# Job scaling on GpSimd and the second four jobs between the first FFN products

## Chip, core and metric

The kernel runs on one core of a Trainium2 chip. The metric is device time in microseconds of one execution. A core has the engines TensorE (PE, with weight loads PEld), VectorE (DVE), ScalarE (ACT) and GpSimd (POOL), each with an instruction queue of its own worked off in order, and SyncE (SP), whose queue issues nearly all DMAs here.

## What is computed

```python
# q, k, v: (8, 8, 576, 64)
scores = q @ k.T / sqrt(64)
gamma  = 1 - 2.0 ** (-5 - arange(8))            # one per head
Dmat   = where(i >= j, gamma ** (i - j), 0)     # decay, causal
x = ((scores * Dmat) @ v)                        # -> (4608, 512)
xn = x / sqrt(mean(x*x, -1) + 1e-6) * rms_g
g  = xn @ w_gate;  val = xn @ w_val              # 512 -> 1536
out = (g * sigmoid(g) * val) @ w_out             # 1536 -> 512
```

Everything is float32 on the chip; the FFN's weights come as float64 and are rounded by the kernel itself, with integer operations.

## The kernel before

**Jobs.** The attention is cut into 32 jobs, one for a batch and a pair of heads (`jobs`), numbered from 0. A sequence of 576 is worked in nine chunks of 64: scores within a chunk and states (k times v of a chunk) by `scores` and `states` on TensorE, decay and causal mask by `weigh` (two L317 instructions on VectorE, to `ret`), a running sum of states by `sums` (L331, L333), then `values` (v times `ret`, L354) and `carried` (sums times q, L374) into the same PSUM banks `av`, and at last x by a multiplication with a table of powers of gamma (L396). `slot(j)` issues `values(j-1)`, `scores(j)`, `states(j)`, `weigh(j)`, `sums(j)` and `carried(j-1)` in an interleaved order; `close(j)` issues the last two parts of a job alone. Between `values` and `carried` stands a tiny instruction that writes `tick` and that the first `carried` product waits for: on POOL for the first eight jobs (L361), on ScalarE from then on (L363).

**First eight jobs (`FIRST`), batches 0 and 1.** `load_first` and `load_tails` bring q, k and v in wide rows into the room of h and of the ring; `turn(j)` transposes q and k on TensorE (L233, L227, L242) and ScalarE copies the result out (L238, L249); `scale_v` multiplies v by powers of gamma on ScalarE (four L265 instructions).

**Later jobs.** `fetch(j)` issues thirteen DMAs on SP: q and k in pieces of 32x32 (`qraw`, `kraw`, one buffer each, so that the next job's load waits for `prepare` of this one), then k, v and vt. `prepare(j)` transposes qraw and kraw on VectorE (two L256) and scales v on ScalarE.

**Norm of a slice of 512 tokens.** `square` (ScalarE), `gather` (VectorE), `norm_1` (means on TensorE L447, r on VectorE, power -0.5 on POOL L453), `diagonals` (four L461), `norm_2` (one product L513 to rb and four L515 on x).

**Weights.** They come in 36 halves, in the order of `halves`: two sets of W_gate/W_val blocks (four halves each), one slice of W_out (four halves), and so on, six sets and three slices. For each, `rounding` issues three steps: the exponent of the next half (one L872 on VectorE, two passes L865 on ScalarE, popped by `act`), the mantissa (L887, L891, L895) and the join (L912). `weights(n)` issues n steps, `weights_to(n)` as many as bring n halves. After a set or slice, POOL builds sums of blocks (L923), and `store_blocks` stores them (L948) to `w_up_blocks` or `w_out_blocks`, from which `refill` loads pieces into the ring (L564). Each join also issues the raw load of the half five further on. From the first FFN product on, exponents and mantissas lie in PSUM banks, which all parts of the kernel share (eight).

**First FFN product of slices 0 and 1.** `up_plain(u, k)` makes four steps of four 128x512 products (L655) for slice u and set k; each step ends in a Silu on ScalarE (even k, L663) or a product with h on VectorE (odd k, L661). Twelve pairs (u, k) make 48 steps, counted by `now`; behind each step the loop in `start` issues what stands at that number: jobs 8 to 11 as `prepare` and `fetch` (28, 36, 41, 44, 46) and `slot` (34, 40, 42, 45), `close(11)` at 47, and weights. After (0, 5), which is step 39, come the rest of the weights, the stores of the last slice of W_out and the first reload, `refill(1)`; after (1, 4), step 43, `refill(2)`.

**Then** `across(0)` and `across(1)` make the second FFN product of slices 0 and 1 (L735), and slices 2 to 8 follow, each with `up` (L594) and `across`; the jobs of the next slice lie between them.

The order of instructions on every engine is that in which `start` issues them (`manual_schedule`); semaphores follow from the tiles. Scores of job j need kT and qT; a step needs the halves of its set.

Of the kernel before, what the change touches and what calls it, by code (L numbers as in the profile page):

```python
# [10 lines left out]
F32 = mybir.dt.float32  # L11
U32 = mybir.dt.uint32
AF = mybir.ActivationFunctionType
ALU = mybir.AluOpType
# [8 lines left out]
def _decay_tables(H, D):  # L23

    pairs = _gamma(H).reshape(H // 2, 2).T
    rows = np.repeat(pairs, D, axis=0)
    pos = np.arange(L)
    p = np.concatenate([pos, pos])  # L30
    gq = rows[:, :, None] ** (pos + L) / np.sqrt(D)
    t = pairs.T[None] ** -p[:, None, None], rows**L, gq, np.roll(gq, D, axis=0)
# [9 lines left out]
def kernel(  # L42
# [67 lines left out]
    gx = const.tile([P, NHP, L], F32, name="gx")  # L110
    gv = const.tile([P, NHP, 2], F32, name="gv")
    gc = const.tile([P, NHP], F32, name="gc")
    tick = const.tile([1, 1], F32, name="tick")
    rms_g = const.tile([P, NHP], F32, name="rms_g")
    rms_k = const.tile([P, NHP], F32, name="rms_k")
# [135 lines left out]
    def prepare(j):  # L251
# [5 lines left out]
            d[nm + "T"] = t  # L257
        scale_v(j)

    def scale_v(j):  # L260
        d = st[j]
        hp = jobs[j][1]
        for e in range(2):
            for t in (d["v"][:, :, e], d["vt"][:, e]):
                nc.scalar.activation(  # L265
                    out=t, in_=t, func=AF.Copy, scale=gv[: t.shape[0], hp, e : e + 1]
                )
# [79 lines left out]
    def values(j):  # L347

        d = st[j]
        av = d["av"] = [bank(f"av_{j}_{i}") for i in range(2)]  # L350
        for c in range(NC):
            i, odd = divmod(c, 2)
            for e in range(2):
                mm = nc.tensor.matmul(  # L354
                    av[odd][column(j, odd, e), i * L : i * L + L],
                    lhsT=d["v"][side(odd), i, e] if c < NC - 1 else d["vt"][:, e],
                    rhs=d["ret"][side(odd), e, i],
                    start=(c < 2), stop=False, skip_group_check=True,
                )
        if j < FIRST:  # L360
            d["valued"] = nc.gpsimd.memset(tick, 0.0)  # L361
        else:
            d["valued"] = nc.scalar.copy(out=tick, in_=mhalf[:1])  # L363
        follow(d["valued"], mm)

    def carried(j):

        d = st[j]
        b, hp = jobs[j]
        av = d["av"]  # L370
        for c in range(1, NC):
            i, odd = divmod(c, 2)
            for e in range(2):
                mm = nc.tensor.matmul(  # L374
                    av[odd][column(j, odd, e), i * L : i * L + L], lhsT=d["sum"][side(e), c - 1],
                    rhs=d["qT"][side(e), c * L : c * L + L],
                    start=False, stop=(c >= NC - 2), skip_group_check=True,
                )
                if c == 1 and e == 0:
                    follow(mm, d["valued"])  # L380
        cut = U // L - b
        for u, c0, c1, o in ((b, 0, cut, b * L), (b + 1, cut, NC, 0)):
            if u not in x_of:
                x_of[u] = xp.tile([P, NHP, U], F32, tag="x", name=f"x_{u}")
            x = x_of[u][:, hp, o : o + (c1 - c0) * L].rearrange("p (c k) -> p c k", k=L)
            for first in (c0, c0 + 1):
                i, odd = divmod(first, 2)
                n = -(-(c1 - first) // 2)
                if n <= 0:
                    continue  # L390
                moves = [(slice(0, P),) * 2]
                if column(j, odd, 0) != side(0):
                    moves = [(side(e), column(j, odd, e)) for e in range(2)]
                for to, at in moves:
                    g = (gq if to == at else gx)[at, hp].unsqueeze(1)
                    nc.vector.tensor_tensor(  # L396
                        out=x[to, first - c0 :: 2],
                        in0=av[odd][at, i * L : (i + n) * L].rearrange("p (c k) -> p c k", k=L),
                        in1=g.to_broadcast([at.stop - at.start, n, L]), op=ALU.mult,
                    )  # L400
        st[j] = {}
# [599 lines left out]
    def start():  # L1001

        nonlocal in_psum
        tables = list(zip((causal, gv, gc, gq, gx), (_causal_table(), *_decay_tables(H, D))))
# [10 lines left out]
        for i in (1, 0, 2):  # L1015
            table(i, nc.scalar)
        for j in range(FIRST):
            load_first(j)
            if j == 0:
                load_tails(0, range(2))  # L1020
                table(3, nc.sync)
            elif j == 1:
                load_tails(0, range(2, H))
                load_half(0, nc.sync)
            elif j in (2, 4, 5, 7):
                load_half({2: 1, 4: 2, 5: 3, 7: 4}[j], nc.sync)
            if j == 3:
                nc.sync.dma_start(out=rms_g, in_=moe_rms_g.rearrange("(c p) -> p c", p=P))
                load_tails(1, range(H))
                table(4, nc.sync)  # L1030
        turn(0, 1)
        scale_v(0)
        squares = []
        for j in range(FIRST):
            slot(j, rest=(j > 0))
            if j + 1 < FIRST:
                turn(j + 1)
            if squares:
                gather(*squares.pop())
            for i in ((1,), (2,), (3,), (4, 5), (6,), (7,), (), ())[j]:  # L1040
                scale_v(i)
            if j:
# [12 lines left out]
        gather(*squares.pop())  # L1055
        fetch(FIRST)
        in_psum = True
        now = 0
        for u, k in (
            (0, 0), (1, 0), (0, 1), (1, 1), (0, 2), (1, 2), (0, 3), (1, 3), (0, 4), (0, 5), (1, 4),  # L1060
            (1, 5),
        ):
            weights_to(READY[k] - 2)
            for i, _ in enumerate(up_plain(u, k)):
                if now == 0:
                    close(FIRST - 1)
# [24 lines left out]
                act(2)  # L1091
                if i == 1:
                    weights_to(READY[k])
                now += 1
            sets_used[k] += 1
            if (u, k) == (0, 5):
                weights_to(len(halves))
                store_blocks(len(halves) + 9)
                refill(1)
            elif (u, k) == (1, 4):  # L1100
                refill(2)
                for f in range(0, NH, 2):
                    differences(0, f)
                inner_sums(0, 0)
                inner_sums(0, 1)
# [82 lines left out]
```

## Time and profile before

| | |
|---|---|
| median of 12 runs | 1151.53 us (1149.22 to 1154.15) |
| the profiled execution | 1151.71 us, span 1149.9 us |
| TensorE busy | 1103.3 us (96%) |
| VectorE, ScalarE, POOL busy | 823.4, 247.5, 399.0 us |
| mean granted TensorE clock | 0.985 |
| slices 0 to 2 of 40 (28.7 us each) | PE busy 8, 7, 8 tenths |
| slice 8 (230 to 259 us) | PE busy 5 tenths |

The span is what the trace shows from the first to the last instruction; the execution's own time has 1.8 us more around it. A row of the timeline has start and duration in us, engine, line, operation, out<-in, count, and in brackets the idle time before it and who ended it. Matmul records come as two to a float32 matmul, so four products of a step are eight records. "issue" as a releaser is a wait that nothing in the profile explains. SPq rows are DMA issues on SP; a DMA lands some us later.

### The profile page before, as it was taken

What the parts mean: (1) busy time and instruction counts of PE and PEld (TensorE: products, weight loads), DVE (VectorE), ACT (ScalarE), POOL (GpSimd) and SP (SyncE); (2) the same over time, 40 slices, a digit from 0 to 9 for tenths busy, and PEclk for the clock granted to TensorE, in tenths of its full rate; (3) what the DMA queues carried; (4) which work ended last, traced back from release to release, by engine and by line L of the source; (5) the groups of instructions that cost most, each with busy time, mean ns of one, the idle gap of its engine ahead of it and who ended that gap; (6) DMA issues with size and microseconds to landing.
All of it is one profiled execution on the core that took longest, in us unless ns stands there. A gap on an engine that the chain in (4) does not pass through costs nothing. (4 is left out here: it accounts for less than half of the span.)

```text
span 1149.9 us, 24145 instructions
## 1 busy us (share of the span) xinstructions
PE 1103.3 (96%) x10086; PEld 919.4 (80%) x10086; DVE 823.4 (72%) x1426; ACT 247.5 (22%) x501; POOL 399.0 (35%) x328
## 2 busy tenths in 40 slices
PE   8789999958999999999999999999999999999997
PEld 6644444437998889888988898889988998898897
DVE  3788979848786778677957794779576944593465
ACT  3633434301102130223012301220122111201110
POOL 0022625534751028201830174016500660173035
PEclk8999999979999999999999999999999999999999
DMA  9645688588886886597768874897576565475461
GB/s 211 161 96 211 229 286 286 171 249 252 312 316 212 232 258 237 167 215 224 263 201 218 249 270 163 201 226 292 186 187 235 193 218 205 150 279 173 156 240 38
DMA packets 255421, 249.22 MB, mean 217 GB/s; under 512 B 193104, under 2 KB 213840, under 8 KB 249168
## 3 DMA queue, kind: packets, MB, share of 16 engines
q1 hardware_dynamic: 253728, 247.11, 68.8%
q8 instruction: 79, 1.29, 0.5%
q10 hardware_dynamic: 1584, 0.56, 0.2%
q14 instruction: 30, 0.25, 0.1%
HBM read 217.55 MB, written 30.08 MB: 215 GB/s over the span
## 5 line engine op out<-in xcount | busy, mean ns | idle before, releaser
L706 POOL TENSOR_TENSOR vi<-h 128x384 f32<-128x384 f32 x64 | 79.6, 1259 | 502.9 <-DVE h L613 453.6
L655 PE MATMUL up<-x,ring 128*128 128x512 f32 x384 | 169.1, 600 | 1.3 <-DVE x L515 0.9
L594 PE MATMUL x<-x,ring 128*128 128x256 f32 x672 | 161.5, 383 | 0.9 <-issue 0.9
L594 PE MATMUL w<-sums,ring 128*128 128x256 f32 x672 | 159.3, 380 | 0.0
L594 PE MATMUL z<-x,ring 128*128 128x256 f32 x672 | 158.7, 379 | 0.0
L655 PEld LDWEIGHTS up<-x,ring 128*128 128x128 f32 x384 | 73.0, 192 | 92.3 <-issue 86.2
L594 PEld LDWEIGHTS z<-x,ring 128*128 128x128 f32 x672 | 127.7, 190 | 19.9 <-issue 2.9
L594 PEld LDWEIGHTS w<-sums,ring 128*128 128x128 f32 x672 | 127.3, 190 | 17.4
L594 PEld LDWEIGHTS x<-x,ring 128*128 128x128 f32 x672 | 125.1, 190 | 18.5 <-issue 1.1
L594 PE MATMUL y<-sums,ring 128*128 128x256 f32 x336 | 79.4, 379 | 0.0
L601 DVE TENSOR_TENSOR h<-u,w 128x512 f32<-128x512 f32 x42 | 28.9, 687 | 65.0 <-PE w L594 48.1
L807 POOL TENSOR_TENSOR vi<-vi 128x512 f32<-128x512 f32 (+1 forms) x56 | 67.1, 1211 | 22.3 <-DVE vi L753 19.7
L594 PEld LDWEIGHTS y<-sums,ring 128*128 128x128 f32 x336 | 63.8, 190 | 8.7
L601 DVE TENSOR_TENSOR u<-m,y 128x512 f32<-128x512 f32 x42 | 28.8, 685 | 50.3 <-PE y L594 50.3
L620 ACT COPY m<-x 128x512 f32<-128x512 f32 x42 | 24.6, 585 | 181.5 <-PE x L594 181.5
L333 DVE SCALAR_TENSOR_TENSOR sum<-sum,gc,s 128x64 f32<-128x64 f32 x192 | 53.9, 281 | 6.8
L615 ACT ACTIVATE h<-h 128x512 f32<-128x512 f32 x63 | 39.5, 629 | 84.0 <-DVE h L601 84.0
L749 ACT COPY vi<-xo 128x512 f32<-128x512 f32 x18 | 10.5, 586 | 207.2 <-PE xo L735 177.6
L923 POOL TENSOR_TENSOR vi<-vi 128x512 f32<-128x512 f32 (+1 forms) x24 | 40.4, 1683 | 35.5 <-DVE vi L912 14.7
L317 DVE SCALAR_TENSOR_TENSOR ret<-s,causal 128x320 f32<-128x320 f32 x64 | 28.8, 484 | 26.7 <-PE s L284 22.3
L601 DVE TENSOR_TENSOR u<-u,z 128x512 f32<-128x512 f32 x42 | 28.8, 687 | 26.7 <-PE z L594 25.7
L923 POOL TENSOR_TENSOR ring<-ring 128x512 f32<-128x512 f32 x24 | 30.5, 1274 | 49.9 <-DMA w_up_blocks<-ring 44.5
(248 smaller groups left out, 2020.1 us busy)
## 6 DMA issues: line engine op xcount, KB each, us to landing
ring<-w_out_blocks SPq DMA_DIRECT2D x63, 1344.0 KB, 6.7
ring<-w_up_blocks SPq DMA_DIRECT2D x42, 1792.0 KB, 7.8
w_out_blocks<-vi SPq DMA_DIRECT2D x21, 448.0 KB, 6.6
out_dram<-vi SPq DMA_DIRECT2D x64, 128.0 KB, 2.9
qraw<-in_q_dram SPq DMA_DIRECT2D x96, 72.0 KB, 5.2
kraw<-in_k_dram SPq DMA_DIRECT2D x96, 72.0 KB, 3.2
k<-in_k_dram SPq DMA_DIRECT2D x48, 128.0 KB, 2.9
v<-in_v_dram SPq DMA_DIRECT2D x48, 128.0 KB, 2.8
```

Source lines behind the costliest of these rows:

```text
L317: nc.vector.scalar_tensor_tensor(out=ret[:, e], in0=s[e][:, : n * L].rearrange("p (c k) -> p c k", k=L), scalar=float(_gamma(H)[2 * hp + e ...
L333: nc.vector.scalar_tensor_tensor(out=t[:, c], in0=t[:, c - 1], scalar=gc[:, hp : hp + 1], in1=part, op0=ALU.mult, op1=ALU.add,)
L594: nc.tensor.matmul(ps[:, i * HU : i * HU + HU], lhsT=w[:, PLACE[blk], c, i * P : i * P + P], rhs=t_of[u][blk][:, c], start=(start and i == ...
L601: nc.vector.tensor_tensor(out=o, in0=a, in1=pairs_of(ps), op=ALU.add)
L615: nc.scalar.activation(out=o, in_=c, func=AF.Silu)
L620: nc.scalar.copy(out=s1, in_=pairs_of(x_))
L655: nc.tensor.matmul(ps, lhsT=w[:, PLACE[blk], c % 2, i * P : i * P + P], rhs=x_of[u][:, c], start=(c == 0), stop=(c == NHP - 1),)
L706: eng.tensor_tensor(out=o, in0=a, in1=b, op=op)
L749: nc.scalar.copy(out=o, in_=ps)
L807: eng.tensor_tensor(out=t[:, :, o], in0=t[:, :, x], in1=t[:, :, y], op=ALU.add)
L923: nc.gpsimd.tensor_tensor(out=t[o], in0=t[x], in1=t[y], op=op)
```

## The change

**Scaling.** For the first eight jobs `scale_first(j)`, on POOL, replaces `scale_v(j)`: four tensor_tensor multiplications in place, on q (by a new table gf that holds the powers that x was multiplied by before), its tail, v and its tail; each has a broadcast second operand. It comes ahead of `turn(j)`, two jobs ahead in most places. x then needs no factor: in `carried`, ScalarE copies `av` to x for j < FIRST, and VectorE does nothing there. `values` writes `tick` for these jobs on VectorE instead of POOL.

**First loads.** gf is the first table on ScalarE's queue; gq and gx come last on SP instead of among the jobs; tails of batch 1 follow job 4, weight halves 0 to 3 follow jobs 2 to 5.

**Order.** Jobs 0 to 3 run as slots and are closed alone; then job 4's slot, the norm of slice 0 and two halves of weights; jobs 5, 6 and 7 stand behind steps 0, 1 and 2 of `up_plain`, `close(7)` behind step 3, the norm of slice 1 behind steps 4 and 5, `fetch(8)` behind step 6. The order of pairs begins (0, 0), (0, 1), (1, 0), (1, 1), not (0, 0), (1, 0), (0, 1), (1, 1). Behind every step stand three weight steps (a whole half), where one stood behind the first four and two or three in turn behind the others. The stores of the last slice of W_out move from behind (0, 5) to behind (1, 4), and so behind `fetch(11)` on SP; both first reloads follow them there, ahead of `fetch(12)`.

```diff
+    def scale_first(j):
+        d = st[j]
+        hp = jobs[j][1]
+        n = NFULL
+        for t, g in (
+            (d["q"], gf[:, hp, :, :n]), (d["qt"], gf[:TAIL, hp, :, n]),
+            (d["v"].rearrange("p c e d -> p e c d"), gv[:, hp].unsqueeze(2)), (d["vt"], gv[:TAIL, hp]),
+        ):
+            g = g.unsqueeze(len(g.shape)).to_broadcast(list(t.shape))
+            nc.gpsimd.tensor_tensor(out=t, in0=t, in1=g, op=ALU.mult)
...
         if j < FIRST:
-            d["valued"] = nc.gpsimd.memset(tick, 0.0)
+            d["valued"] = nc.vector.memset(tick, 0.0)
...
                 for to, at in moves:
+                    if j < FIRST:
+                        nc.scalar.copy(
+                            out=x[:, first - c0 :: 2],
+                            in_=av[odd][:, i * L : (i + n) * L].rearrange("p (c k) -> p c k", k=L),
+                        )
+                        continue
...
-        turn(0, 1)
-        scale_v(0)
-        squares = []
-        for j in range(FIRST):
+        scale_first(0)
+        turn(0, 1)
+        scale_first(1)
+        for j in range(NHP):
             slot(j, rest=(j > 0))
-            if j + 1 < FIRST:
-                turn(j + 1)
             if squares:
                 gather(*squares.pop())
-            for i in ((1,), (2,), (3,), (4, 5), (6,), (7,), (), ())[j]:
-                scale_v(i)
             if j:
-                squares.append((*divmod(j - 1, NHP), square(*divmod(j - 1, NHP))))
-            act(1)
-            if j == 5:
-                norm_1(0)
-            elif j == 6:
-                norm_2(0)
-            weights((0, 0, 1, 2, 2, 2, 1, 2)[j])
-            if j == 4:
-                gather(*squares.pop())
-            elif j == 5:
-                diagonals(0)
-            act(1)
+                squared(0, j - 1)
+            turn(j + 1)
+            scale_first(j + 2)
+        weights(2)
+        close(NHP - 1)
         gather(*squares.pop())
-        fetch(FIRST)
+        squared(0, NHP - 1)
+        act(1)
+        slot(NHP, rest=False)
+        gather(*squares.pop())
+        norm_1(0)
+        diagonals(0)
+        turn(NHP + 1)
+        scale_first(NHP + 2)
+        norm_2(0)
+        weights(5)
+        act(1)
         in_psum = True
         now = 0
         for u, k in (
-            (0, 0), (1, 0), (0, 1), (1, 1), (0, 2), (1, 2), (0, 3), (1, 3), (0, 4), (0, 5), (1, 4),
+            (0, 0), (0, 1), (1, 0), (1, 1), (0, 2), (1, 2), (0, 3), (1, 3), (0, 4), (0, 5), (1, 4),
             (1, 5),
         ):
             weights_to(READY[k] - 2)
             for i, _ in enumerate(up_plain(u, k)):
-                if now == 0:
+                if now < 3:
+                    j = NHP + 1 + now
+                    slot(j)
+                    if squares:
+                        gather(*squares.pop())
+                    squared(1, now)
+                    if j + 1 < FIRST:
+                        turn(j + 1)
+                        if j + 2 < FIRST:
+                            scale_first(j + 2)
+                elif now == 3:
                     close(FIRST - 1)
-                    gather(1, NHP - 1, square(1, NHP - 1))
-                elif now == 1:
+                    gather(*squares.pop())
+                    squared(1, NHP - 1)
+                elif now == 4:
+                    gather(*squares.pop())
                     norm_1(1)
-                elif now == 2:
                     diagonals(1)
-                elif now == 3:
+                elif now == 5:
                     norm_2(1)
+                elif now == 6:
+                    fetch(FIRST)
...
-                weights((3 - now % 2) if now > 3 else 1)
+                weights(3)
                 act(2)
...
-            if (u, k) == (0, 5):
+            if (u, k) == (1, 4):
                 weights_to(len(halves))
                 store_blocks(len(halves) + 9)
-                refill(1)
-            elif (u, k) == (1, 4):
                 refill(2)
```

More of the change, by code (lines that the diff above doesn't have):

```diff
@@ L31, in _decay_tables @@
     gq = rows[:, :, None] ** (pos + L) / np.sqrt(D)
-    t = pairs.T[None] ** -p[:, None, None], rows**L, gq, np.roll(gq, D, axis=0)
+    n = 4
+    at = np.stack([(n * np.arange(2 * L) + c) % L for c in range(n)] + [p], axis=1)
+    g = _gamma(H).reshape(1, H // 2, 2, 1)
+    gf = g ** (at[:, None, None] + L) / np.sqrt(D)
+    t = pairs.T[None] ** -p[:, None, None], rows**L, gq, np.roll(gq, D, axis=0), gf
     return [np.ascontiguousarray(x).astype(np.float32) for x in t]
@@ L112 @@
     gc = const.tile([P, NHP], F32, name="gc")
+    gf = const.tile([P, NHP, 2, NFULL + 1], F32, name="gf")
     tick = const.tile([1, 1], F32, name="tick")
@@ L1003, in start @@
         nonlocal in_psum
-        tables = list(zip((causal, gv, gc, gq, gx), (_causal_table(), *_decay_tables(H, D))))
+        tables = list(zip((causal, gv, gc, gq, gx, gf), (_causal_table(), *_decay_tables(H, D))))
         def table(i, queue):
@@ L1014, in start @@
         warm_up(6)
-        for i in (1, 0, 2):
+        for i in (5, 1, 0, 2):
             table(i, nc.scalar)
@@ L1018, in start, with squared @@
             load_first(j)
[L1019 to L1026, printed above, removed]
+            if j < 2:
+                load_tails(0, (range(2), range(2, H))[j])
+            elif j < 6:
+                load_half(j - 2, nc.sync)
+            elif j == 7:
+                load_half(4, nc.sync)
             if j == 3:
                 nc.sync.dma_start(out=rms_g, in_=moe_rms_g.rearrange("(c p) -> p c", p=P))
+            elif j == 4:
                 load_tails(1, range(H))
-                table(4, nc.sync)
+        table(3, nc.sync)
+        table(4, nc.sync)
+        squares = []
+        def squared(u, c):
+            squares.append((u, c, square(u, c)))
+        scale_first(0)
         turn(0, 1)
-        scale_v(0)
-        squares = []
-        for j in range(FIRST):
+        scale_first(1)
+        for j in range(NHP):
             slot(j, rest=(j > 0))
-            if j + 1 < FIRST:
-                turn(j + 1)
             if squares:
                 gather(*squares.pop())
-            for i in ((1,), (2,), (3,), (4, 5), (6,), (7,), (), ())[j]:
-                scale_v(i)
             if j:
-                squares.append((*divmod(j - 1, NHP), square(*divmod(j - 1, NHP))))
-            act(1)
-            if j == 5:
-                norm_1(0)
-            elif j == 6:
-                norm_2(0)
-            weights((0, 0, 1, 2, 2, 2, 1, 2)[j])
-            if j == 4:
-                gather(*squares.pop())
-            elif j == 5:
-                diagonals(0)
-            act(1)
-        gather(*squares.pop())
-        fetch(FIRST)
+                squared(0, j - 1)
[3 more added lines that the diff above has]
+        close(NHP - 1)
+        gather(*squares.pop())
+        squared(0, NHP - 1)
[9 more added lines that the diff above has]
+        act(1)
         in_psum = True
```

## Prediction

> **What bounds the kernel now.** I read the busy time by stretch first, then the order of time on TensorE, then the issues on SP. (Columns of the first view: stretch in us, its length, busy us and instructions of PE, PEld, DVE, ACT, POOL, then granted clock, DMA share, GB/s.)
>
> ```profile
> 0.00:62.60 62.60, 50.95 (x1252) 43.30 (x1253) 35.98 (x117) 29.91 (x78) 2.88 (x14) 0.89 0.74 179
> 62.60:100.10 37.50, 33.78 (x144) 15.65 (x143) 32.47 (x63) 13.19 (x21) 6.96 (x7) 0.95 0.51 138
> 100.10:240.60 140.50, 138.01 (x657) 63.44 (x655) 122.42 (x227) 49.41 (x85) 66.37 (x46) 1.00 0.70 239
> 240.60:268.50 27.90, 13.38 (x226) 8.33 (x225) 9.85 (x23) 3.15 (x10) 6.77 (x7) 0.76 0.97 217
> 268.50:1149.90 881.40, 867.21 (x7817) 788.67 (x7812) 622.68 (x998) 151.79 (x307) 316.06 (x256) 1.00 0.69 219
> ```
>
> From 268.5 on (start of the first `across`) TensorE is 98% busy and the diff leaves everything as it is. So the question is only when `across(0)` begins. Ahead of it stand the eight first jobs (to 62.6) and 48 steps of `up_plain`.
>
> ```profile
> 86.34 106.67 PE L655 MATMUL up<-x,ring 128*128 128x512 f32 x248 [0.93 <-DVE x L515]
> 241.14 0.28 PE L354 MATMUL av<-ret,vt 64*64 64x64 f32 x4
> 254.23 1.34 PE L284 MATMUL s<-qT,kT 64*64 64x64 f32 x40 [12.81 <-DVE kT L256]
> 267.87 0.69 PE L374 MATMUL av<-qT,sum 64*64 64x64 f32 x32 [1.38 <-ACT tick L363]
> ```
>
> Eight records are a step: 106.67/31 = 3.44 us, without a gap for 31 steps. Counting back, step 8 begins at 100.1. The one large hole is 12.81 us ahead of the scores of job 11 (counted from 0).
>
> ```profile
> 212.02 1.01 SPq L948 DMA_DIRECT2D w_up_blocks<-ring  x2
> 233.48 6.01 SPq L948 DMA_DIRECT2D w_out_blocks<-vi  x7
> 239.60 1.08 SPq L564 DMA_DIRECT2D ring<-w_out_blocks  x1
> 240.73 4.82 SPq L159 DMA_DIRECT2D qraw<-in_q_dram  x4
> 245.65 4.37 SPq L159 DMA_DIRECT2D kraw<-in_k_dram  x4
> ```
>
> To see here: SP stood from 213 to 233.48 at the stores of the last weight slice (a wait of 19.7 us for POOL's L923, whose last sum ends at 233.46); job 11's raw loads were queued behind it, and then took 12.2 us to issue behind the stores and the reload, against 7.0 for job 8 at 174.4. TensorE ran dry on kT.
>
> **What the Trainium skill says.** "SBUF — State Buffer", Who interferes with whom: a VectorE instruction in a two-port mode, or with two SBUF inputs, is blocked by a GpSimd one that reads SBUF. The trace agrees: the four diagonals (L461) take 0.87 us at 56.49 with POOL idle and 2.90 at 79.00 under its L923; a join (L912) 0.69 and 1.30. "GPSIMD Engine Reference", 3.1 Elementwise: about 2.6 cycles an element at 1.2 GHz, 1.1 us for 512; the trace has 1.26 to 1.28 (L923, 128x512). "DMA: Bandwidth & Descriptors", Anatomy of one DMA: a semaphore wait happens on the issuing sequencer; that is the queue above.
>
> **The change, part by part.** Times are from the start of the span; durations are those of rows of the trace before. The units: a step is 3.44 us of TensorE. A slot is 3.35 there (values 0.7, scores 0.75, states 0.75, carried 1.15, rows from 44.2 to 48.4), a turn 2.1 (1.1, 0.65, 0.35), a close 1.85. On VectorE a slot is 3.3 (two L317 0.88, L331 0.21, seven L333 2.14, read from 64.31 to 67.53), a half of weights with the next exponent 3.2 (90.73 to 93.97), L661's product or a gather 0.6.
>
> *Scaling on POOL.* Each job has two 128x512 products (1.26 us) and two of 64x128 (estimate 0.4): 3.3 us, 27 us in all, in place of four ScalarE activations (1.6 us). ScalarE gets the copies to x (about 1.2 us a job by its other PSUM copies, 0.58 for 512 columns), VectorE loses 0.9. A slot takes 5.2 us (values of job 1 at 24.25, of job 2 at 29.46), so POOL keeps up. It puts 1.3 us ahead of the first turn, hidden: the second job's tails land only at 13.6 to 14.4, where TensorE waits now (1.56 and 0.51). The gq table leaves SP ahead of job 1 (0.6), the wait for ScalarE's v goes (0.3). Values of job 2 then start at 28.5 instead of 29.46. The added broadcast product isn't in the trace: bounds 1.1 (skill) and 2.5 us (twice L923); I take 1.26.
>
> *First four closed alone.* Onward: carried(2) ends 31.6; turn(4) 4.5 (its 2.37 us issue gap kept) 36.1; close(3) 2.5: 38.6; scores and states of job 4 2.1: 40.7; VectorE's ret and sums 3.3 from 39.8: 43.1; gather 0.6, mean squares 1.05, r 0.15, POOL's power 1.4: 46.4. The diagonals now meet POOL scaling jobs 6 and 7: between 0.87 and 2.90, I take 2.90: 49.3. rb 1.05, x 2.7: 53.1. Only then, in VectorE's order, come mantissa and join of halves 0 and 1: 2.5 + 0.35 + 2.5 = 5.4: 58.5 =: J. The first FFN product starts at 55.7 instead of 62.6: 6.9 us won.
>
> *Steps 0 to 7, with jobs 5 to 7 between them.* TensorE and VectorE now wait for each other in turn, so I go through their orders with the units above. Set 1 follows set 0 at once, so halves 4 to 7 are due early. Counted from J: step 0 ends 1.75 (its last two products need half 1), slot 5 and turn 6 7.2, step 1 10.65, slot 6 and turn 7 16.3. (Half 2's second exponent pass stands on ScalarE behind turn 6's copies: half 2 at 11.8, wanted at 16.3.) VectorE: job 6's ret and sums from 12.1 to 15.4, half 3 at 18.6; step 2 needs it: ends 20.3. Slot 7 23.7, copies of x (the bank) 24.9, step 3 28.3, close(7) 30.2. VectorE: job 7 25.1, gather, half 4 28.9, gather, half 5 32.9: step 4 ends 36.3. Gather, mean squares 38.6; step 5 42. Power, diagonals 41.2, half 6 44.4, L661's product 0.6, x 2.7, half 7 50.9: step 6 ends 52.6, step 7 56. So step 8 begins at 58.5 + 56 = 114.5, not 100.1. Of the 56 us, 27.5 are steps, 18 slots, turns, close, and about 11 waits for VectorE, which has some 37 us of work here and often waits in turn. The tick of these jobs moves from POOL to VectorE, behind a half; the carried products wait for it at most 0.3 us.
>
> *Steps 8 to 40.* Now each step carries a whole half: VectorE 3.2 us, with L661's product 3.8, against 3.44. Rounding ends by step 33 and not in slot 9. TensorE may lead by three steps (banks), so of 12 steps at +0.36, two transposes (1.5) and a raw load late by about 2 us behind the stores of a slice I charge 3.5 (0 to 7). The raw loads of job 8, moved from ahead of step 0 behind step 6 on SP, are wanted at step 28, some 75 us later: nothing. So are the tables, rms_g, tails and weight halves that change places among the first loads: the same bytes, but gq, ahead of the same consumers. End of step 40: 114.5 + 33 x 3.44 + 1.4 (slot 8) + 3.5 = 232.9 =: A.
>
> *Stores behind the raw loads.* Slot 9's VectorE work ends 7.2 after A, its qT frees qraw at A+7.9, job 11 is issued in 7.0 (as at 174.4:181.4) and in time for A+18: the 12.81 us go. But the stores follow at A+14.9, then two reloads, and job 12 behind these. In the profile, stores to v landed took 254.8 - 233.5 = 21.3 with one reload; the second is 1344 KB, at some 400 GB/s 3.4 more: job 12's v at A+39.6, scaled at A+41.3. TensorE comes to carried(11) after 3 slots of 2.3, 7 steps and values 0.8: A+31.7. ScalarE's tick, for which carried(11) waits, stands in ScalarE's queue behind that scaling (the 1.38 us above is this wait). Stall 9.6 us; bounds 0 and 14. VectorE is held in job 12's transposes meanwhile; behind it stand a product, x and the differences, which wait for carried(11) anyway. `across(0)` begins at 232.9 + 41.3 + 0.6 = 274.8 instead of 268.5: +6.3. Its own first wait stays: VectorE's chain from carried(11) to L768 (11 us) is the same. The reload moved here, and its fellow, land near A+29 and A+32.5, well ahead of it. (In the profile this part, from the end of step 40 at 215.1, takes 53.4 us with 2.3 of waits for VectorE in slot 9; now 41.9.)
>
> **Sum** against the profiled execution (1151.71, of which the span is 1149.9): start -6.9, steps 0 to 7 +21.3 (58.8 for 37.5), steps 8 to 40 +3.4 (118.4 for 115.0), the rest -11.5: +6.3, 1158.0. The median of the runs is 0.2 lower: 1157.8.
>
> **Rivals.** (1) Faster: the hole is not replaced. If the stores drain while jobs 11 and 12 load and v of job 12 is there by A+30, the stall is 0: 1157.8 - 9.6 = 1148.2. It decides once job 12 lands 6.3 us earlier than I reckon. For: the unhindered load takes 7 us, the queue is freed earlier; against: 12.2 us of issue behind one reload in the profile, and a WAR on qraw. Steps 0 to 7 some 7 us quicker would only bring it to zero. (2) No difference: steps 0 to 7 lose only 15 us, because VectorE is less often in turn with TensorE than I laid out, and all else holds: 1151.5. (3) Slower still: POOL's broadcast product takes twice L923; then 6 us a job exceed the 5.2 of a slot, four slots lose 1.4 each: 1163.5. For: POOL's rows vary from 1.26 to 1.8; against: these are larger.
>
> **How the numbers follow.** Forecast 0.46, (1) 0.18, (2) 0.16, (3) 0.20. Faster 0.18, same 0.16, slower 0.66 by 0.2% (2.3 us), about what a measurement of this kernel can tell. Unknowns: diagonals -2, pacing -3.5 to +3.5, stall -9.6 to +4.4, issue gaps -3.6, POOL +5.7. The best of them alone is (1), the worst (3) with 2.5 us more; so 1147 to 1166 leaves out about 2 in 10. The forecast's own range is 1154 to 1163.
>
> **What would show it.** In the profile after: first L655 product at 54 to 58; step 8 not before 110; no wait for kT of job 11, but one of 5 us or more of the av products for tick, with ScalarE's v waiting for the DMA of job 12; `across(0)` at 270 to 280. Wrong would be step 8 near 105, or no such wait.

## The result, and the profile after

The changed kernel takes 1174.01 us (median of 8 runs, 1171.04 to 1177.63) against 1151.31 us (32 runs): 1.0199 times as long, 95% interval 1.0186 to 1.0213. The forecast was 1157.8 (1147 to 1166): slower was right, and the time is 16 us above it. The profiled execution took 1172.08 us, its span is 1170.0.

The stretches are cut at the same events as in the forecast: first FFN product, start of step 8, end of step 40, `across(0)`. (Busy time by stretch, changed kernel; columns as in the table of before.)

```profile
0.00:60.05 60.05, 37.81 (x788) 30.48 (x789) 29.34 (x79) 17.36 (x46) 24.46 (x39) 0.84 0.72 169
60.05:119.90 59.85, 49.13 (x606) 26.83 (x607) 40.97 (x88) 20.55 (x48) 11.18 (x9) 0.93 0.37 112
119.90:244.31 124.41, 118.67 (x337) 51.30 (x335) 102.88 (x178) 45.59 (x76) 60.52 (x40) 0.99 0.76 246
244.31:287.99 43.68, 33.35 (x545) 18.66 (x544) 25.22 (x64) 7.29 (x20) 7.86 (x8) 0.91 0.72 199
287.99:1170.00 882.01, 868.50 (x7816) 789.83 (x7812) 621.66 (x998) 151.92 (x307) 317.83 (x256) 1.00 0.69 219
```

| stretch | before | forecast | after | forecast change | measured change |
|---|---|---|---|---|---|
| to the first FFN product | 62.6 | 55.7 | 60.05 | -6.9 | -2.5 |
| steps 0 to 7 | 37.5 | 58.8 | 59.85 | +21.3 | +22.4 |
| steps 8 to 40 | 115.0 | 118.4 | 124.4 | +3.4 | +9.4 |
| end of step 40 to `across(0)` | 53.4 | 41.9 | 43.7 | -11.5 | -9.7 |
| from `across(0)` on | 881.4 | 881.4 | 882.0 | 0 | +0.6 |

So all but 0.6 us of the loss lies ahead of `across(0)`, as forecast. Two rows are off by 4 to 6 us (the first and the third), one by 1.8. The columns are single profiles, and the start varies in them: in ten profiles with this code up to the means of slice 0, these means begin between 43.4 and 47.3 us (43.57 here), and in four with the code of before the first FFN product begins between 60.5 and 64.1. The order of time on TensorE shows the waits (changed kernel; start, duration, instruction, and in brackets the idle time before it and its releaser; L678 is the FFN product, L935 a join, L391 `carried`).

```profile
52.58 2.04 PE L536 MATMUL rb<-diag,ones 128*128 128x512 f32 x2 [3.83 <-DVE diag L484]
60.05 6.13 PE L678 MATMUL up<-x,ring 128*128 128x512 f32 x8 [5.43 <-DVE ring L935]
...
113.17 79.32 PE L678 MATMUL up<-x,ring 128*128 128x512 f32 x180 [4.42 <-DVE ring L935]
...
201.70 7.54 PE L678 MATMUL up<-x,ring 128*128 128x512 f32 x16 [1.46 <-DVE ring L935]
...
220.77 0.68 PE L321 MATMUL s<-v,k 64*64 64x64 f32 x28 [3.38 <-DVE sums L918]
...
286.93 1.13 PE L391 MATMUL av<-qT,sum 64*64 64x64 f32 x32 [10.33 <-ACT tick L380]
```

The first product waits for VectorE's join, not for x. Of the 180 records of the third line 12 are the end of step 6 and step 7; step 8 begins at 119.9. The last line is the stall that was forecast at `carried(11)`, 9.6 us there, 10.33 here; no wait for kT of job 11 is left. On VectorE two rows matter (changed kernel, the same columns):

```profile
46.75 5.68 DVE L484 TENSOR_SCALAR diag<-ident,r 128x128 f32<-128x128 f32 x4 [1.15 <-POOL r L476]
...
102.54 0.87 DVE L484 TENSOR_SCALAR diag<-ident,r 128x128 f32<-128x128 f32 x4 [1.14 <-POOL r L476]
...
218.11 0.69 DVE L895 TENSOR_SCALAR exp<-ring 128x512 uint32<-128x512 uint32 x1 [4.67 <-DMA ring<-in_moe_w_out_dram]
```

The same four diagonals take 5.68 us for slice 0 and 0.87 for slice 1. One by one (both slices; shortest, median and longest in ns) they show where the time went:

```profile
L484 DVE TENSOR_SCALAR diag<-ident,r x8: 273/284/4146, 46.7 to 103.1; 128x128 f32<-128x128 f32 x8
```

The longest is the second of slice 0: it starts at 47.7 and takes 4.15 us. Beside the diagonals of slice 0 stand GpSimd's eight scaling products of jobs 6 and 7, without a gap (changed kernel, POOL; the first row, the last row):

```profile
46.68 1.05 POOL L275 TENSOR_TENSOR ring<-ring,gf 128x512 f32<-128x512 f32 x1
...
51.76 0.39 POOL L275 TENSOR_TENSOR vi<-vi,gv 64x128 f32<-64x128 f32 x1
```

A 128x512 product takes 1.05 us, a tail 0.39: the forecast's rival of a slow broadcast product (2.5 us) is out. Its lower bound of 1.1 us, an estimate from the rate in the Trainium skill ("GPSIMD Engine Reference", 3.1 Elementwise), is near what was measured. The third VectorE row waits for the last raw half. Its place in SP's order of issues (changed kernel; L881 is a raw half, L164 q and k of a job, L971 stores):

```profile
187.34 6.13 SPq L971 DMA_DIRECT2D w_out_blocks<-vi  x7
...
197.83 8.17 SPq L164 DMA_DIRECT2D qraw<-in_q_dram  x4
206.10 4.31 SPq L164 DMA_DIRECT2D kraw<-in_k_dram  x4
...
213.35 0.54 SPq L881 DMA_DIRECT2D ring<-in_moe_w_out_dram  x1
...
259.96 6.26 SPq L971 DMA_DIRECT2D w_out_blocks<-vi  x7
266.32 2.33 SPq L587 DMA_DIRECT2D ring<-w_out_blocks  x2
268.70 8.13 SPq L164 DMA_DIRECT2D qraw<-in_q_dram  x4
276.92 4.26 SPq L164 DMA_DIRECT2D kraw<-in_k_dram  x4
```

Job 9's loads were issued behind seven stores (three raw halves and two more stores lie between), took 15 us, and the raw half came after them. In the kernel before they stood ahead of these stores:

```profile
174.41 1.96 SPq L159 DMA_DIRECT2D qraw<-in_q_dram  x4
...
183.64 5.42 SPq L948 DMA_DIRECT2D w_out_blocks<-vi  x7
```

The same picture comes again at 260: stores, two reloads, then job 12's loads; ScalarE shows who pays (changed kernel):

```profile
285.06 0.51 ACT L282 ACTIVATE v<-v,gv 128x256 f32<-128x256 f32 x1 [17.51 <-DMA v<-in_v_dram]
...
286.70 0.17 ACT L380 COPY tick<-mhalf 1x1 f32<-1x1 f32 x1
```

### The profile page after: what moved, and what is told of

Same layout as the page of the kernel before. It is cut to its first block, busy times and chain, and to the rows that moved or that the text cites. A ratio compares the mean times of both kernels' runs of the same rounds, so it can differ in the third digit from the quotient of the medians.

```text
span 1170.0 us, 24183 instructions
## 1 busy us (share of the span) xinstructions
PE 1107.5 (95%) x10086; PEld 917.1 (78%) x10086; DVE 820.1 (70%) x1406; ACT 242.7 (21%) x497; POOL 421.9 (36%) x352
## 5 line engine op out<-in xcount | busy, mean ns | idle before, releaser
L678 PE MATMUL up<-x,ring 128*128 128x512 f32 x384 | 175.7, 614 | 16.4 <-DVE ring L935 15.0
L678 PEld LDWEIGHTS up<-x,ring 128*128 128x128 f32 x384 | 73.3, 195 | 112.7 <-issue 94.1
L334 DVE SCALAR_TENSOR_TENSOR ret<-s,causal 128x320 f32<-128x320 f32 x64 | 28.5, 485 | 29.0 <-PE s L301 15.8
```

The costliest lines, as they stand in the source:

```text
L334: nc.vector.scalar_tensor_tensor(out=ret[:, e], in0=s[e][:, : n * L].rearrange("p (c k) -> p c k", k=L), scalar=float(_gamma(H)[2 * hp + e ...
L678: nc.tensor.matmul(ps, lhsT=w[:, PLACE[blk], c % 2, i * P : i * P + P], rhs=x_of[u][:, c], start=(c == 0), stop=(c == NHP - 1),)
```

## The experiments

Each run's ratio is to the kernel before on the same chip, with its 95% interval; "us" is that ratio's difference from 1 times 1151.5, so the changed kernel stands at +22.9. Single profiled executions of one kernel differ by 2 us and more, so totals are taken from the ratios and only stretches from the profiles.

**Is the order or the scaling the cost?**

```diff
 # e5_order_alone: the changed kernel with
-        scale_first(0); turn(0, 1); scale_first(1)
+        turn(0, 1); scale_v(0); scale_v(1)
 # scale_v for scale_first throughout, tick on GpSimd, x times its table on VectorE
 # e6_scaling_alone: start() of before, with
-        turn(0, 1); scale_v(0)
+        scale_first(0); turn(0, 1); scale_first(1)
 # scale_first(j + 2) behind turn(j + 1); ScalarE's copies to x, tick on VectorE
```

> The changed kernel with the scaling taken back: v is scaled on ScalarE, x multiplied by its table on VectorE and tick written on GpSimd for the first eight jobs, as before; the new order of jobs, norms, weights, pairs and stores stays. My theory: the loss is in the order (second four jobs, weight halves and norm among the first eight steps, a half with every step, the stores), so this run is slow too: the scaling brings the first slots some 3 to 5 us forward and costs about 4 beside the diagonals, which nearly cancel: 1170 to 1178. The rival (GpSimd's scaling and what it blocks on VectorE is the cost): below 1160.

> The kernel before with the scaling alone: GpSimd scales q and v of the first eight jobs ahead of their turns, ScalarE copies x, VectorE writes tick; order, weights, pairs and stores as before. My theory: in the first 62 us ScalarE loses some 1.6 us of scaling per job and gains 1.2 of copies, slots get shorter by about half a us each, and the joins and mantissas beside GpSimd's 23 us of products get longer by some us; 1148 to 1153 (within 3 us of the kernel before). The rival (the scaling is what costs): above 1156.

The order alone: 1178.74 us, 1.0227 (1.0206 to 1.0247), +26.1 us, slow as my theory had it and 0.7 us above its range. The scaling alone: 1154.87 us, 1.0035 (1.0020 to 1.0051), +4.0, just above my range and below the rival's (22 runs from 1150.5 to 1163.2, the widest spread here; by the medians +2.7). The cost is in the order. In the old order the scaling takes some 3 to 4 us; in the new one the kernel with it is 3 us faster than without, which the intervals do not separate.

**The diagonals.** Two runs put the scaling of jobs 6 and 7 elsewhere.

```diff
 # e4_scaling_held: GpSimd's first scaling of job 6 waits for
+        held.append(norm_2(0))          # the last x product of slice 0
         scale_first(NHP + 2)
-        norm_2(0)
 # e8_scaling_behind_joins: it waits for the join of half 1
-        scale_first(NHP + 2)
         norm_2(0)
         weights(5)
+        scale_first(NHP + 2)            # follows joined[-1]
```

> The changed kernel, but GpSimd's scaling of job 6 (and so of job 7) starts only when x of slice 0 is normed on VectorE, so that GpSimd is idle beside the four diagonals. My theory: the diagonals take 0.9 us instead of 5.7, the first two joins come 4 to 5 us earlier, and this carries through to the end less 1 to 2 us for the joins that now lie beside the scaling: 1169 to 1172. The rival (VectorE and GpSimd only meet elsewhere, or another wait fills the place): 1173 to 1175. If the held scaling makes turn(6) late, step 0's neighbours show a wait for GpSimd and the time is above 1175.

> The changed kernel, but GpSimd's scaling of jobs 6 and 7 starts only when the second half of weights is joined, so that neither the diagonals nor the first two halves lie beside it; VectorE then stands idle for some 4 us and reads PSUM. My theory, after the run that held the scaling to the norm: it only moved the 5 us from the diagonals to the first mantissa and join; here they go, the second join ends at 57 to 59 instead of 62.9, and 3 to 5 us are carried to the end: 1169 to 1171. The rival (what VectorE loses here, it would have waited for anyway in steps 0 to 7): 1173 to 1175.

e4: 1174.30 us, 1.0193 (1.0173 to 1.0212): no gain; my theory missed, and the rival had it. e8: 1170.84 us, 1.0150 (1.0128 to 1.0172): 5.6 us below the changed kernel by the ratios, 3.2 by the medians. VectorE in e4 (diagonals, then mantissa and join of half 0; lines are moved by 4 or 5):

```profile
48.56 0.87 DVE L488 TENSOR_SCALAR diag<-ident,r 128x128 f32<-128x128 f32 x4 [1.14 <-POOL r L480]
...
57.09 3.51 DVE L923 SCALAR_TENSOR_TENSOR ring<-ring 128x512 f32<-128x512 uint32 x1
60.63 1.41 DVE L940 SCALAR_TENSOR_TENSOR ring<-ring,t 128x512 f32<-128x512 f32 x1
```

The diagonals were freed, and the mantissa's last part took 3.51 us instead of 0.69, the join 1.41 instead of 0.69: the block moved 9 us on and cost the same. In e8, where GpSimd is idle beside all of them (VectorE):

```profile
48.51 0.87 DVE L486 TENSOR_SCALAR diag<-ident,r 128x128 f32<-128x128 f32 x4 [1.15 <-POOL r L478]
...
56.38 0.69 DVE L920 SCALAR_TENSOR_TENSOR ring<-ring 128x512 f32<-128x512 uint32 x1
57.11 0.69 DVE L939 SCALAR_TENSOR_TENSOR ring<-ring,t 128x512 f32<-128x512 f32 x1
```

From the means (L470 and its like) to the first FFN product it is 12.45 us (45.50 to 57.95) against 16.48 (43.57 to 60.05); the five other profiles with this part unchanged have 16.0 to 16.5, and e5, which has no such run on GpSimd, 12.3. To the last wait ahead of step 8 it is 65.7 us against 69.6, so the gain is carried that far; beyond, only the totals show it, since e8's profile was taken of a run 2.5 us above its median.

**Steps 0 to 7.** One run leaves VectorE work out, one moves TensorE's.

```diff
 # e12_four_halves_unrounded: halves 4 to 7
-            mantissa(i)
+            if i not in range(4, 8):
+                mantissa(i)             # exponent(i) likewise
 # e10_job_under_norm
         norm_1(0)
-        diagonals(0)
         turn(NHP + 1)
         scale_first(NHP + 2)
+        slot(NHP + 1)
+        diagonals(0)
 ...                                     # jobs 6 and 7 behind steps 0 and 1
```

> The changed kernel with work left out: halves 4 to 7 of the weights (the second set) are not rounded; their exponent, mantissa (four VectorE instructions and two ScalarE passes each) are gone and one VectorE instruction of the same size copies the upper words in place of the join. My theory: in steps 0 to 7 TensorE waits for VectorE in turn, and these 11 us of VectorE are on the path: step 8 begins 6 to 11 us earlier counted from the join of the second half, 1163 to 1168. The rival (the norm's chain and TensorE's own work set these steps, the halves lie in VectorE's idle time): step 8 less than 3 us earlier, 1171 to 1175.

> The changed kernel, but job 5's slot and job 6's turn stand on TensorE under the norm of slice 0 and no longer behind step 0; jobs 6 and 7 follow behind steps 0 and 1, close(7) behind step 2, the norm of slice 1 as in the changed kernel. Here TensorE has no work from the end of carried(3) to the first FFN product but slot 4, the means, a turn and rb. My theory: TensorE's 6.6 us of slot and turn fit into that hole, VectorE's 3.3 us for the slot come ahead of the diagonals, so the first FFN product starts 2 to 4 us later and step 8 some 3 to 5 us earlier: 1169 to 1171. The rival (VectorE alone sets the pace up to step 8, wherever TensorE's work lies): step 8 within 2 us of where it is, 1172 to 1176.

e12: 1167.28 us, 1.0132 (1.0117 to 1.0146), 7.7 us below the changed kernel for 11 us of VectorE work. e10: 1174.73 us, 1.0198 (1.0182 to 1.0215), no gain; its rival was right. TensorE, last wait ahead of step 8, e12:

```profile
107.65 79.26 PE L678 MATMUL up<-x,ring 128*128 128x512 f32 x180 [2.30 <-DVE ring L940]
```

and e10:

```profile
62.43 6.58 PE L678 MATMUL up<-x,ring 128*128 128x512 f32 x8 [5.43 <-DVE ring L935]
...
113.88 80.53 PE L678 MATMUL up<-x,ring 128*128 128x512 f32 x180 [4.34 <-DVE ring L935]
```

From the first product to this row it is 53.1 us in the changed kernel and 47.7 in e12; step 8 begins 5.3 us earlier, a little less than the 6 to 11 of my theory. In e10 a slot and a turn (6.6 us of TensorE) are gone from these steps, the first product comes later, and the row starts at 113.88 as if nothing had been moved (113.17; counted from the means 69.5 us against 69.6): VectorE's order sets these steps, wherever TensorE's work lies. (e12 also takes eight ScalarE passes away, and no run parts the two; that it is VectorE is read from the waits, which end with a join.)

**Steps 8 to 40.**

```diff
 # e7_pace
-                weights(3)
+                weights(3 if now < 8 else 3 - now % 2)
 # e13_fetch_alone; e9_pace_fetch has both
-                elif now == 28:
+                elif now == 20:
                     prepare(FIRST)
                     fetch(FIRST + 1)
```

> The changed kernel, but from step 8 on two and three weight steps stand in turn behind the steps of the first FFN product, as before the change, not three each time. My theory: VectorE then needs about 3.2 us a step and not 3.8, so the steps from 8 to 40 go at 3.44 us again and the wait of VectorE for the last raw half is no longer on the path: step 40 ends 7 to 10 us earlier counted from step 8 (116 to 119 in place of 125.9), and the rest follows: 1164 to 1168. The rival (the pace is set by TensorE or by transfers, and fewer weight steps only lengthen the work behind step 39): 1171 to 1176.

> The changed kernel with the transposes of job 8 and the loads of job 9 behind step 20 in place of step 28, and three weight steps behind every step as in the changed kernel. Of the some 10 us that steps 8 to 40 lost, the pace alone gave 2 back and pace and loads together 10. My theory: the queue on SP is the larger part (a wait of 4.7 us of VectorE and 3.4 us of TensorE for slot 8 behind it), the pace of 3.84 us per half on VectorE the smaller (22 steps at 3.525 instead of 3.44, and waits of 0.2 to 1.5 us): the loads alone give 4 to 6 us, 1168 to 1170. The rival (the two are one: at three steps each time VectorE is late anyway and the load fills its wait): 1171 to 1174.

> The changed kernel with two and three weight steps in turn from step 8 on, and with the transposes of job 8 and the loads of job 9 behind step 20 instead of step 28. The run with the pace alone kept TensorE at 3.44 us a step up to slot 8, but there VectorE waited 7.25 us for a raw half whose load stood on SP behind the loads of job 9 and the stores of the second W_out slice. My theory: with job 9's loads out of that place the wait falls below 2 us, step 40 ends 117 to 120 us after step 8 began (125.9 in the changed kernel), and the rest follows: 1164 to 1167. The rival (the raw half is late by the stores alone, or the transfers bound this stretch): VectorE still waits 4 us or more for it, 1170 to 1173.

| | us | ratio | steps 8 to 40 |
|---|---|---|---|
| changed | 1174.01 | 1.0199 (1.0186 to 1.0213) | 124.4 |
| e7, pace | 1172.10 | 1.0175 (1.0152 to 1.0198) | 124.5 |
| e13, loads of job 9 | 1170.70 | 1.0175 (1.0156 to 1.0194) | 119.8 |
| e9, both | 1164.33 | 1.0112 (1.0095 to 1.0130) | 115.0 |

(The last column counts from the start of step 8, 12 records behind the wait for the last join, to the values of slot 9; six other runs that leave this part as it is have 122.3 to 125.5, so it varies by 3 us. The 125.9 of the expectations counts from a point 1.5 us earlier.) The pace alone gives nothing in this stretch, where my theory said 7 to 10. The loads alone give 4.6, within the 4 to 6 of my theory and 2.5 below the shortest of the six. By the totals each alone gives 2.8 us, hardly told from the changed kernel; both together give 10.0. In e7 VectorE has less to do in a step, but fewer halves are done when job 9's loads go out; it is now an earlier raw half of the last slice that stands behind both these loads (issued from 198.5 on) and the stores (206.2), and the wait grew (VectorE, e7):

```profile
222.13 0.69 DVE L895 TENSOR_SCALAR exp<-ring 128x512 uint32<-128x512 uint32 x1 [7.25 <-DMA ring<-in_moe_w_out_dram]
```

In e13 no such wait is left (the longest for a raw half is 1.64 us), but TensorE still waits for joins, 0.2 to 1.4 us at a time, from 174 on. With both, one row holds 28.5 steps with no wait (TensorE, e9), and the stretch takes the 115.0 us of the kernel before:

```profile
112.88 99.62 PE L678 MATMUL up<-x,ring 128*128 128x512 f32 x228 [4.42 <-DVE ring L935]
```

**The stores and job 12.**

```diff
 # e2_before_stores: the kernel before with
             if (u, k) == (0, 5):
                 weights_to(len(halves))
-                store_blocks(len(halves) + 9)
-                refill(1)
             elif (u, k) == (1, 4):
+                store_blocks(len(halves) + 9)
                 refill(2)
 # e1 (changed kernel) and e3 (e2's kernel): behind the differences of slice 1,
 # and no longer behind step 46
+        prepare(FIRST + 4)
+        fetch(FIRST + 5)
 # e11_before_reloads_first: e2's kernel with
         refill()
+        fetch(FIRST + 4)                # no longer behind step 44
 ...
+            if i == 5:                  # within across(0)
+                prepare(FIRST + 4)
+                fetch(FIRST + 5)
```

> The kernel before with one part of the change alone: the stores of the last W_out slice and both first reloads stand behind pair (1, 4), behind the loads of job 11 and ahead of those of job 12. My theory: the 12.81 us ahead of job 11's scores go and 8 to 11 us come back ahead of carried(11), as a wait for ScalarE's tick behind job 12's v: 1147 to 1150 (1.5 to 4.5 us below the kernel before). The rival (the hole isn't replaced, as my forecast's first rival had it): 1138 to 1141. The other rival (the moved stores cost more than the hole): above 1152.

> The changed kernel, but job 12's transposes and the scaling of its v stand behind the differences of slice 1, ahead of across(0), and the loads of job 13 behind them. My theory: the 10.3 us ahead of carried(11) are ScalarE's tick standing behind the scaling of job 12's v, which waits for a load queued behind the stores. Then the wait for tick goes (below 1 us), across(0) begins near 277.7 instead of 288.0, and of the 10.3 us some 1 to 4 come back as a wait of across(0) for the first reload or for VectorE: 1164 to 1168. The rival (the late transfers themselves bound this part, the tick was only the first to meet them): across(0) waits 8 us or more for its first reload, and the time stays at 1171 to 1174.

> The kernel before with the stores and reloads moved as in the run beside it, and also job 12's transposes and v's scaling behind the differences of slice 1. My theory: neither the wait for kT of job 11 (12.81 us) nor the wait for tick is left; what comes back is 1 to 4 us of across(0) waiting for its first reload or for VectorE: 1139 to 1143. The rival (the transfers bound the part whoever waits for them): across(0) waits 8 us or more, 1147 to 1150.

> The kernel before with the stores of the last W_out slice and the first reloads moved as in the changed kernel, but now all reloads stand on SP ahead of job 12's loads, and job 12's transposes, v's scaling and job 13's loads come only behind the fifth part of across(0). In the run with job 12 only prepared later, across(0) waited 4.1 and 5.3 us for reloads that were issued behind job 12's and job 13's small pieces. My theory (the order on SP, not the bytes, made these late): neither a wait for kT of job 11, nor for tick, nor more than 2 us for reloads is left: 1137 to 1142. The rival (the bytes bound it, stores and reloads take their time in any order): across(0) waits 8 us or more, 1146 to 1149.

e2: 1146.73 us, 0.9942 (0.9926 to 0.9959), 0.3 us better than the range I expected: the moved stores alone are a gain. The wait for tick of job 11 is 10.81 us there, in the place of 12.81 for kT and 1.38 for tick. e1: 1177.26 us, 1.0216 (1.0200 to 1.0231), slower than either theory had it. e3: 1147.89 us, 0.9956 (0.9938 to 0.9973), the rival's range; its waits for reloads are 4.13 and 5.30 us. TensorE in e1:

```profile
280.02 0.69 PE L391 MATMUL av<-qT,sum 64*64 64x64 f32 x32 [0.34 <-ACT tick L380]
...
294.62 2.90 PE L758 MATMUL wo<-ring,h 128*128 128x128 f32 x12 [4.33 <-DMA ring<-w_out_blocks]
...
307.05 2.55 PE L758 MATMUL yo<-ring,h 128*128 128x128 f32 x12 [4.65 <-DMA ring<-w_out_blocks]
```

The wait for tick went, as I had said, and 9.0 us came back in `across(0)`, with 1 to 1.3 us more in the products behind each wait (2.90 and 2.55 us; 1.58 and 1.50 in the changed kernel); from `across(0)` to the end e1 takes 894.5 us for 882.0. So the stall at `carried(11)` had covered late reloads. The third was issued behind job 12's loads (287.42), the others behind job 13's (300.10). e11 puts reloads first: 1140.72 us, 0.9911 (0.9889 to 0.9933), 10.2 us below the kernel before, the best version of this study. One wait of 4.28 us for a reload is left in `across(0)`, more than the 2 us expected, and from there to the end e11 takes 887.8 us for 881.4 in the kernel before, so 6.4 us still come back (TensorE, e11):

```profile
248.79 0.69 PE L374 MATMUL av<-qT,sum 64*64 64x64 f32 x32 [0.35 <-ACT tick L363]
...
268.03 2.90 PE L735 MATMUL yo<-ring,h 128*128 128x128 f32 x12 [4.28 <-DMA ring<-w_out_blocks]
```

**Do the causes add up?** e14 is the changed kernel with the edits of e8, e9 and e11.

> The changed kernel with three mends together: GpSimd's scaling of jobs 6 and 7 behind the second join (3 us by itself), pace and place of job 9's loads (10 us), all first reloads ahead of job 12's loads on SP and job 12 prepared within across(0) (11 us in the kernel before). My theory: these are three separate losses of the changed kernel at three places, so they add: 1174.0 - 3.2 - 9.7 - 9 to -11 = 1150 to 1152.5, and what is left against the same mend in the kernel before (1140.7) is the steps 0 to 7. The rival (a later wait takes up part of what an earlier mend gives): 1155 to 1162.

1155.93 us, 1.0047 (1.0027 to 1.0066), +5.4 us: outside my range, in the rival's. But my sum was wrong: I took e11's whole gain on the kernel before, of which the moved stores, which the changed kernel has already, are 6.7 (e2). The reloads' own part is 10.2 - 6.7 = 3.5. With it: 22.9 - 5.6 - 10.0 - 3.5 = 3.8, and 5.4 (3.1 to 7.6) was measured. They add within what can be told (each term is known to 2 or 3 us, and e11's part holds the late preparation of job 12 too). What is left against e11 is 15.6 us by the ratios; in the two profiles, which lie 20.4 us apart, step 8 begins at 120.8 and 97.8, and after it e14 is not slower. That is the remaining price of the new order up to step 8.

## Why the prediction was wrong in size

**First four closed alone: too good by 4.4 us.** In this profile the slots came as forecast: GpSimd's power ended at 46.7 (46.4 forecast), although the slots took another course; that it is this near is in part luck, since other profiles of this code come up to 3.7 us later. The failed term is "the diagonals now meet POOL scaling jobs 6 and 7: between 0.87 and 2.90, I take 2.90". It measured 5.68, outside both ends, because the upper end came from one row of the kernel before (2.90, from 79.00) with three GpSimd products beside it (79.15 to 83.16), and here eight stand back to back. The other 1 us is rb (2.04 instead of 1.05: the granted clock was 0.50 there, behind 3.83 us of idle; in e10, behind 1.03 us, rb took 1.10 at 1.00). The joins that follow took what was forecast. The place in the Trainium skill that the forecast used ("SBUF — State Buffer", Who interferes with whom) says that the one which comes later is blocked, not slowed; the trace agrees, and adds that it can be blocked through more than one instruction: one diagonal took 4.15 us (shortest 0.27), through six GpSimd products that follow each other, and the four ended at 52.43, the run of eight at 52.15. (In the kernel before the diagonals got through before the run beside them ended; what decides that is open.) e4 and e8 show the block by moving the run.

**Steps 0 to 7: right.** 59.85 us for 58.8, counted from the join of half 1 57.0 for 56; TensorE was idle for 10.7 of them, where the forecast had about 11. That VectorE's order is the limit was argued there, and e12 and e10 show it from both sides.

**Steps 8 to 40: the step that failed most.** The forecast charged 3.5 (0 to 7) for pace, two transposes and "a raw load late by about 2 us behind the stores of a slice". The stretch came out at 124.4 for 118.4, so the charge should have been 9.5. Both parts were seen and both mis-sized: the raw load was late by 4.67 and not 2, since the halves now run ahead and job 9's loads, which the diff doesn't touch, come to stand on SP between the stores and the last raw half; and VectorE at 3.84 us a half leaves TensorE no lead to take it up (3.38 us at slot 8, 1.46 and less before). I had laid the new pace beside the steps and not beside the queue of SP. e9 shows that these two are all of it; with the pace alone taken back (e7) all of the 9.4 us stay, with the loads alone (e13) 4.8. One term the forecast did not have: TensorE's waits in this stretch are 5.3 us, and what follows a wait is slower. The six steps behind slot 8 took 22.5 us instead of 20.6, with a granted clock of 0.81 from 217 to 225.

**Stores behind the raw loads: right, off by 1.8 us.** Stores 15.65 us after the end of step 40 (14.9 forecast), v of job 12 at +40.75 (39.6), the stall 10.33 (9.6). (The row at 174.4, which the forecast calls job 8's, is job 9's; its 7.0 us hold.) That the stall is ScalarE's tick behind v's scaling is shown by e1, which takes it away. What the forecast did not see, and what lay within its numbers only by luck, is that the reloads stand behind the stall: without it they bind.

**Rivals.** (1), the hole isn't replaced, is refuted by the 10.33 us; (2), only 15 us in steps 0 to 7, by 22.4; (3), slow GpSimd products, by 1.05 us. The range missed 1174 because both wrong terms went past their bounds in one direction. Between the forecast's sum and the profiled execution 14.1 us are open: 4.4 + 1.1 + 6.0 + 1.8 + 0.6 = 13.9 of them are in the table; the median is 1.9 above that execution.

Not settled: why e6 is some 3 to 4 us slower than the kernel before (its first FFN product begins 1.4 us later, less than profiles of the kernel before differ by; GpSimd waits there for q, up to 3.8 us, ahead of turns), and why steps 8 to 40 vary by 3 us between runs of the same code.

## What to carry to other kernels

When a change moves weights or other background work ahead, lay its new times beside every in-order queue that feeds it: a load that isn't touched can come to stand behind a burst of stores that it used to precede. A wait that is taken away may have covered a later one on the same transfers; ask what lands when without it, and put on the queue first what is wanted first. A price that is bounded from one overlapping row is bounded only for that overlap: ask how long the other engine's run is, not how long one of its instructions is.

## What the runs showed of the hardware that I had not expected

- Four VectorE instructions of 128x128, 0.87 us alone, took 5.68 us under a run of eight GpSimd products, and ended 0.3 us after the run's end (52.15); a single one of them took 4.15 us. When the run was moved (e4), it stretched one VectorE instruction with two SBUF inputs from 0.69 to 3.51 us.
- Four loads of q in pieces of 32x32 take 1.95 us to issue on a quiet queue and, in the runs with the new order, 7.5 to 8.4 behind seven stores of 448 KB or two reloads of 1344 KB.
- The products right behind an idle of 4 to 5 us were slower: twelve records of 128x128 in 2.90 and 2.55 us (e1, granted clock 0.50 and 0.58) for 1.58 and 1.50 in the changed kernel (1.00 where they took 1.58).
